# Causal attention and two gated products on one core: banks of the transposes and of the result, and the step at which the result is split

## The chip, the cores and the metric

The kernel runs on one core of a Trainium2 chip. The metric is the device time of one execution in microseconds (us): 584.55 us is the median of three runs before the change. TensorE (PE, with its weight loads as PEld), VectorE (DVE), ScalarE (ACT), GpSimd (POOL) and SyncE (SP, which issues the DMAs) each have a queue of their own and work through it in the order in which the program wrote it.

## The reference

Two batches, 12 heads, 448 tokens, head dimension 64; all in float32.

```python
scores = scale * (q @ k.T)                    # per head, causal mask
attn   = exp(scores - max) / (sum + 1e-9)
x      = concat_heads(attn @ v)               # 896 x 768
h = x @ w_in;  g = h * cos(h);  y = g @ w_out           # 768 -> 2048 -> 768
c = (y @ w_a) * (y @ w_b);      out = c @ w_out2        # 768 -> 1536 -> 768
```

## The kernel before

**Products.** Each large product is computed from activations and weights that are split into a high and a low part (`x_hi`, `x_lo` and so on), three matmuls for a term. They fill the time from about 90 us to the end.

**Attention.** The twelve units of work are pairs of heads, numbered 0 to 11 here (six pairs in each batch). A pair is done in four banks of scores (`BANKS`): the first holds tiles 6 and 0 (448 and 64 columns), the second tiles 4 and 2 (320 and 192), the third tile 5 (384), the fourth tiles 3 and 1 (256 and 128). One bank is one step of a loop that is written out by hand: `CYCLE` names each function with the step, counted from the pair's own, at which it is issued, and within a step the functions are issued in the order of the list. No scheduler moves anything after that.

For pair n, with its first step at 4n, the functions are:

- `scores` (L339, TensorE): matmuls of two banks, two steps ahead. Tile 6 (448 columns, first bank) comes first and tile 4 (320 columns, second bank) next.
- `row_max` (L362, VectorE): reads a bank of scores, adds the mask, writes the scores into one of two buffers `p` (`N_P = 2`, L298) and takes the row maximum. It frees the bank. Behind each stands a short read of the accumulator (`mn`).
- `exps` (L383, ScalarE): exponentials in `p`, with row sums. `recip` (L390, L391, VectorE): reciprocals of the sums. `scale_p` (L398, GpSimd): multiplies the rows.
- `transposes(n, odd)` (L412, TensorE): seven transposes of 128x128 into two banks, four in the first and three in the second; the even group at step 4n+5, the odd one at 4n+7.
- `keep(n, odd)` (L423 ScalarE, L425 VectorE): copies both banks into `pp`, one bank on each of the two engines.
- `values(n)` (L439, TensorE) at step 4n+10: the product with `v` into the bank `xa`.
- `x_hi(n)` (L449, ScalarE) and `x_lo(n)` (L454, VectorE): split `xa` into its high and its low part; `x_lo` is the last to read the bank.

The weights of the first product are prepared at fixed steps between these (L100, L105, L111, L118 and, on GpSimd, L129 and L138).

The eight banks of the accumulation memory are shared out by `BUFS`: four for scores (`s`), two for transposes (`t`), two for the result (`x`). The products later take all eight in turn, in the order of the tags.

Of the kernel before, what the change touches and what calls it, by code (L numbers as in the profile page):

```python
# [26 lines left out]
def tile_causal_attention_cos_gate_bilinear(  # L27
# [35 lines left out]
    def act_tiles(pool, tag, kind, b, n):  # L63
        return [
            tuple(pool.tile([P, S], F32R, tag=f"{tag}{b}_{t}{part}", name=f"{kind}{b}_{t}{part}") for part in ("hi", "lo"))
            for t in range(n)
        ]
# [89 lines left out]
    x = [act_tiles(xy, "xy", "x", b, NPAIR) for b in range(B)]  # L157

    psum = ctx.enter_context(tc.tile_pool(name="psum", bufs=1, space=PSUM))
    BUFS = {"s": 4, "t": 2, "x": 2}  # L160
    cycle = itertools.cycle([tag for tag, n in BUFS.items() for _ in range(n)])

    def bank(tag, name):
        return psum.tile([P, 512], F32, tag=tag, name=name, bufs=BUFS[tag])

# [113 lines left out]
    with ExitStack() as actx:  # L279
# [183 lines left out]
        def at(fn, i):  # L463
# [15 lines left out]
            (values, 10),  # L479
            (transposes, 5, 0),  # L480
            (transposes, 7, 1),
            (x_hi, 12),
            (x_lo, 13),
            (load_qk, -10),
            (load_v, -2),
        ]
# [131 lines left out]
```

## Time and profile before

| | |
|---|---|
| Runs | 584.55 us median of 3 (584.34 to 584.56) |
| Profiled execution | 584.54 us, of which the span of the trace is 582.7 |
| TensorE busy | 573.5 us, 98% of the span |
| VectorE, ScalarE, GpSimd busy | 360.7, 267.0, 221.4 us |
| TensorE clock granted | full in every slice |

Times of rows count from the start of the span. A busy time says that instructions were in flight on an engine; matmuls are pipelined, and where one waits while another is still in flight the row stays busy. "[0.66 <-POOL p L398]" behind a row says that the engine stood idle for 0.66 us before it, until the named instruction let it go on.

### The profile page before, as it was taken

What the parts mean: (1) busy time and instruction counts of PE and PEld (TensorE: products, weight loads), DVE (VectorE), ACT (ScalarE), POOL (GpSimd) and SP (SyncE); (2) the same over time, 40 slices, a digit from 0 to 9 for tenths busy, and PEclk for the clock granted to TensorE, in tenths of its full rate; (3) what the DMA queues carried; (4) which work ended last, traced back from release to release, by engine and by line L of the source; (5) the groups of instructions that cost most, each with busy time, mean ns of one, the idle gap of its engine ahead of it and who ended that gap; (6) DMA issues with size and microseconds to landing.
All of it is one profiled execution on the core that took longest, in us unless ns stands there. A gap on an engine that the chain in (4) does not pass through costs nothing.

```text
span 582.7 us, 8735 instructions
## 1 busy us (share of the span) xinstructions
PE 573.5 (98%) x3310; PEld 513.1 (88%) x3310; DVE 360.7 (62%) x599; ACT 267.0 (46%) x531; POOL 221.4 (38%) x200
## 2 busy tenths in 40 slices
PE   8899999999999999999999999999999999999997
PEld 6566688999999999999999999999999999999996
DVE  4888765777777774654465666666666666655400
ACT  5797847777777733232223433333333333222100
POOL 4756662666666652232132222222222222322200
PEclk9999999999999999999999999999999999999999
DMA  8671511233333334423242333333333333444000
GB/s 312 263 220 58 183 44 67 87 117 114 114 103 99 100 109 137 144 91 109 91 162 102 117 109 109 108 109 108 110 108 110 109 109 109 139 141 139 33 33 32
DMA packets 15450, 67.80 MB, mean 116 GB/s; under 512 B 1712, under 2 KB 3376, under 8 KB 15408
## 3 DMA queue, kind: packets, MB, share of 16 engines
q1 hardware_dynamic: 15408, 67.25, 34.4%
q8 instruction: 26, 0.43, 0.3%
q14 instruction: 16, 0.13, 0.1%
HBM read 64.49 MB, written 2.75 MB: 115 GB/s over the span
## 4 chain that ended last, share of the span: by engine, by line
PE 94%; DVE 2%; ACT 2%; POOL 1%; issue 1%; DVEq 0%; POOLq 0%
PE h L175 20%; PE y L175 20%; PE o L175 15%; PE a L175 15%; PE b L175 15%; PE xa L439 3%; PE pt L412 3%; PE s L339 2%; ACT p L383 2%; DVE p L362 1%; PE warm L459 1%; POOL p L398 1%; DVE pp L425 0%; POOL w_lo L138 0%; DVE w_raw L118 0%
## 5 line engine op out<-in xcount | busy, mean ns | idle before, releaser
L138 POOL TENSOR_TENSOR w_lo<-w_raw,w_hi 128x768 fp32r<-128x768 f32 (+1 forms) x70 | 128.9, 1841 | 264.8 <-ACT w_hi L131 194.1
L111 DVE SCALAR_TENSOR_TENSOR w_raw<-w_raw 128x768 int32<-128x768 int32 (+1 forms) x70 | 124.1, 1772 | 63.2 <-ACT w_raw L100 62.3
L131 ACT ACTIVATE w_hi<-w_raw 128x768 fp32r<-128x768 f32 (+1 forms) x67 | 59.9, 895 | 163.2 <-DVE w_raw L118 100.0
L118 DVE SCALAR_TENSOR_TENSOR w_raw<-w_raw 128x768 int32<-128x768 int32 (+1 forms) x70 | 65.9, 941 | 0.4
L100 ACT ACTIVATE w_raw<-w_raw 128x768 f32<-128x768 f32 (+1 forms) x70 | 61.4, 877 | 0.0
L398 POOL TENSOR_SCALAR p<-p,sums 128x448 f32<-128x448 f32 (+6 forms) x84 | 42.5, 527 | 27.3 <-DVE sums L391 16.9
L383 ACT ACTIVATE p<-p,mn 128x448 f32<-128x448 f32 (+6 forms) x84 | 41.8, 499 | 15.7 <-DVE mn L362 15.7
L105 DVE TENSOR_SCALAR w_raw<-w_raw 128x768 int32<-128x768 int32 (+1 forms) x70 | 42.7, 610 | 0.0
L362 DVE CUSTOM_DVE_ANT_0 p<-s,mask 128x448 f32<-128x448 f32 (+6 forms) x84 | 31.9, 416 | 13.1 <-PE pt L412 8.0
L215 DVE SCALAR_TENSOR_TENSOR r<-k,h 128x448 f32<-128x448 int32 x32 | 19.7, 617 | 26.0 <-ACT k L214 25.6
L568 DVE COPY o<-o 128x448 f32<-128x448 f32 x12 | 7.5, 625 | 35.3 <-PE o L175 35.3
L339 PE MATMUL s<-qk_raw 64*64 64x64 f32 (+6 forms) x336 | 28.5, 410 | 0.3 <-DVE mn L362 0.2
L412 PE MATMUL pt<-ident,p 128*128 128x128 f32 x168 | 23.7, 279 | 3.9 <-POOL p L398 2.2
L214 ACT ACTIVATE k<-h 128x448 int32<-128x448 f32 x32 | 17.3, 539 | 18.5 <-PE h L175 17.7
L339 PEld LDWEIGHTS s<-qk_raw 64*64 64x64 f32 x336 | 15.7, 139 | 11.3 <-issue 4.4
L412 PEld LDWEIGHTS pt<-ident,p 128*128 128x128 f32 x168 | 18.1, 140 | 7.5 <-POOL p L398 3.1
L560 DVE TENSOR_TENSOR c<-a,bs 128x448 f32<-128x448 f32 x24 | 15.0, 625 | 15.4 <-PE a L175 15.4
L439 PE MATMUL xa<-pp,v 128*64 128x64 f32 (+3 forms) x336 | 23.8, 293 | 0.0
L439 PEld LDWEIGHTS xa<-pp,v 128*64 128x64 f32 x336 | 16.1, 137 | 8.7 <-issue 6.8
L231 DVE SCALAR_TENSOR_TENSOR r<-r,h 128x448 f32<-128x448 f32 x32 | 19.5, 610 | 1.5 <-ACT r L226 1.5
L221 ACT ACTIVATE r<-r 128x448 f32<-128x448 f32 x32 | 18.3, 571 | 0.0
L226 ACT ACTIVATE r<-r 128x448 f32<-128x448 f32 x32 | 18.2, 569 | 0.0
(377 smaller groups left out, 1564.6 us busy)
## 6 DMA issues: line engine op xcount, KB each, us to landing
w_raw<-in_w_in SPq DMA_DIRECT2D x16, 768.0 KB, 4.3
w_raw<-in_w_out SPq DMA_DIRECT2D x12, 768.0 KB, 4.3
w_raw<-in_w_b SPq DMA_DIRECT2D x12, 768.0 KB, 4.2
w_raw<-in_w_a SPq DMA_DIRECT2D x12, 768.0 KB, 4.3
w_raw<-in_w_o SPq DMA_DIRECT2D x12, 768.0 KB, 4.3
v<-in_v SPq DMA_DIRECT2D x12, 448.0 KB, 5.4
qk_raw<-in_qk SPq DMA_DIRECT2D x11, 448.0 KB, 5.7
w_raw<-in_w_out SPq DMA_DIRECT2D x6, 512.0 KB, 3.8
```

Source lines behind the costliest of these rows:

```text
L100: nc.scalar.activation(high, high, ACTF.Copy, scale=2.0**-112)
L105: nc.vector.tensor_single_scalar(low, low, 29, op=ALU.logical_shift_right)
L111: nc.vector.scalar_tensor_tensor(out=low, in0=high, scalar=3, in1=low, op0=ALU.logical_shift_left, op1=ALU.bitwise_or)
L118: nc.vector.scalar_tensor_tensor(out=low, in0=high, scalar=SIGN, in1=low, op0=ALU.bitwise_and, op1=ALU.bitwise_or)
L131: nc.scalar.activation(pair[0][:, :n], src, ACTF.Copy)
L138: engine.tensor_tensor(out=lo[:, :n], in0=f32(raw.pop(i)[:, :, 0]), in1=f32(hi)[:, :n], op=ALU.subtract)
L175: nc.tensor.matmul(ps, w[:, c * P : (c + 1) * P], acts[t + c][part], start=t == 0 and i == 0, stop=t + k == n and i == len(terms) - 1,)
L339: nc.tensor.matmul(T["s", i + c][q, o : o + WIDTH[j]], t[h, Q_COL[j] : Q_COL[j] + D], t[h, FIRST[j] : FIRST[j] + WIDTH[j]], start=True, st ...
L383: nc.scalar.activation(t, t, ACTF.Exp, bias=T["mn", n][:, c], scale=-1.0, accum_out=row_sum(n, j))
L398: nc.gpsimd.tensor_scalar(out=t, in0=t, scalar1=row_sum(n, j), scalar2=1.0, op0=ALU.mult, op1=ALU.mult)
L412: nc.tensor.transpose(dst, p_bufs[n % N_P][:, o : o + P], ident)
L439: nc.tensor.matmul(ps[e * D : (e + 1) * D, o * D : w * D], t[:, k, e], p[:, :, :, q].rearrange("p s l q -> p (s l) q") if k < 3 else p[:, ...
```

## The change

One bank moves from the result to the transposes, and both halves of the split are issued one step sooner.

```diff
-    BUFS = {"s": 4, "t": 2, "x": 2}
+    BUFS = {"s": 4, "t": 3, "x": 1}
...
             (transposes, 5, 0),
             (transposes, 7, 1),
-            (x_hi, 12),
-            (x_lo, 13),
+            (x_hi, 11),
+            (x_lo, 12),
```

VectorE, around the row maxima of pair 5 (`p1_116`, scores `s_501` and the next bank) before the change; `pt_550` is the second bank of pair 3's odd transposes, `x0_2lo` the low part of pair 2's result:

```order
L391 RECIPROCAL sums_498<-sums_498 128x3
L425 COPY pp_512<-pt_550 128x3x128
L362 ISA p1_116,mn_554<-s_501,mask_101 128x320
L362 ISA mn_554 128x1
L362 ISA p1_116,mn_554<-s_501,mask_101 128x192
L362 ISA mn_554 128x1
L454 TENSOR_TENSOR x0_2lo_76<-xa_516,x0_2hi_75 128x448
L362 ISA p1_116,mn_554<-s_558,mask_101 128x384
```

The same place on VectorE after the change:

```order
L391 RECIPROCAL sums_498<-sums_498 128x3
L425 COPY pp_512<-pt_550 128x3x128
L454 TENSOR_TENSOR x0_2lo_76<-xa_516,x0_2hi_75 128x448
L362 ISA p1_116,mn_555<-s_501,mask_101 128x320
L362 ISA mn_555 128x1
L362 ISA p1_116,mn_555<-s_501,mask_101 128x192
L362 ISA mn_555 128x1
L362 ISA p1_116,mn_555<-s_559,mask_101 128x384
```

The low part has moved from behind the row maxima of 320 and 192 columns to a place ahead of them, right behind the copy of the transposes. The same holds for every pair that has row maxima there.

ScalarE at the same pair before the change (`pt_545` is the first bank of pair 3's odd transposes):

```order
L383 ACTIVATE p0_115,sums_498<-p0_115,mn_462 128x128
L423 ACTIVATE pp_512<-pt_545 128x4x128
L383 ACTIVATE p1_116,sums_555<-p1_116,mn_554 128x448
L383 ACTIVATE p1_116,sums_555<-p1_116,mn_554 128x64
L449 ACTIVATE x0_2hi_75<-xa_516 128x448
L383 ACTIVATE p1_116,sums_555<-p1_116,mn_554 128x320
```

And after it:

```order
L383 ACTIVATE p0_115,sums_498<-p0_115,mn_463 128x128
L449 ACTIVATE x0_2hi_75<-xa_516 128x448
L423 ACTIVATE pp_512<-pt_545 128x4x128
L383 ACTIVATE p1_116,sums_556<-p1_116,mn_555 128x448
L383 ACTIVATE p1_116,sums_556<-p1_116,mn_555 128x64
L383 ACTIVATE p1_116,sums_556<-p1_116,mn_555 128x320
```

The high part now stands ahead of the copy of the odd transposes and of two exponentials.

TensorE's queue holds the same instructions in the same order; what an instruction waits for has changed. Pair 2's even transposes before the change (`Activation_49`, `DVE_49`, `Pool_49` and `PE_49` are the counters of ScalarE, VectorE, GpSimd and TensorE):

```order
L412 MATMUL pt_488<-ident_66,p1_116 128x2x64 [waits Activation_49,Pool_49]
L412 MATMUL pt_488<-ident_66,p1_116 128x2x64
L412 MATMUL pt_488<-ident_66,p1_116 128x128
L412 MATMUL pt_488<-ident_66,p1_116 128x2x64
L412 MATMUL pt_493<-ident_66,p1_116 128x128 [waits DVE_49,PE_49]
```

And after it:

```order
L412 MATMUL pt_489<-ident_66,p1_116 128x2x64 [waits Pool_49]
L412 MATMUL pt_489<-ident_66,p1_116 128x2x64
L412 MATMUL pt_489<-ident_66,p1_116 128x128
L412 MATMUL pt_489<-ident_66,p1_116 128x2x64
L412 MATMUL pt_494<-ident_66,p1_116 128x128 [waits Activation_49]
```

The first transpose no longer waits for a copy, only for the scaled rows; the fifth waits for ScalarE's copy instead of VectorE's.

## Rows read from the trace of the kernel before

**Rows 1.** Busy time by stretches: stretch, its length, busy time (instructions) of PE first

```profile
30.00:40.00 10.00, 10.00 (x124) 7.03 (x124) 8.57 (x38) 9.18 (x33) 6.34 (x14) 1.00 0.77 252
...
90.00:580.00 490.00, 488.63 (x2417) 452.53 (x2413) 295.65 (x338) 203.51 (x323) 168.89 (x99) 1.00 0.32 105
```

**Rows 2.** Waits of PE: for whom, us in total, times, longest

```profile
PE pt L412 <- POOL p L398: 2.2, 3, 0.9
PE pt L412 <- ACT pp L423: 1.0, 2, 0.5
...
PE pt L412 <- DVE pp L425: 0.6, 2, 0.4
```

**Rows 3.** Timeline of PE, from pair 3's odd transposes to pair 4's

```profile
33.97 0.98 PE L412 MATMUL pt<-ident,p 128*128 128x128 f32 x7
...
36.66 1.23 PE L339 MATMUL s<-qk_raw 64*64 64x448 f32 x16
...
37.82 1.98 PE L439 MATMUL xa<-pp,v 128*64 128x384 f32 x28
...
39.73 0.98 PE L412 MATMUL pt<-ident,p 128*128 128x128 f32 x7
```

**Rows 4.** Score matmuls (L339) in flight, PE first; pairs 4, 6 and 11

```profile
25.20:25.28 0.08, 0.00 (x1) 0.01 (x1) 1.00 1.83 768
25.20:25.30 0.10, 0.02 (x4) 0.03 (x4) 1.00 1.46 614
...
36.68:36.80 0.12, 0.12 (x2) 0.12 (x4) 1.00 0.38 149
36.80:36.82 0.02, 0.02 (x4) 0.02 (x4) 1.00 0.88 358
...
68.12:68.23 0.11, 0.11 (x2) 0.11 (x4) 1.00 0.00 0
68.23:68.25 0.02, 0.02 (x4) 0.02 (x4) 1.00 0.00 0
```

**Rows 5.** Timeline of DVE in the same turn

```profile
35.10 0.22 DVE L362 CUSTOM_DVE_ANT_0 p<-s,mask 128x64 f32<-128x64 f32 x1 [1.09 <-PE pt L412]
...
35.54 0.53 DVE L425 COPY pp<-pt 128x384 f32<-128x384 f32 x1
...
35.98 0.48 DVE L362 CUSTOM_DVE_ANT_0 p<-s,mask 128x320 f32<-128x320 f32 x1
...
36.67 0.08 DVE L362 DVE_READ_ACCUMULATOR2_ANT mn<- 128x1 f32 x1
36.70 0.62 DVE L454 TENSOR_TENSOR x_2lo<-xa,x_2hi 128x448 fp32r<-128x448 f32 x1
...
37.24 0.55 DVE L362 CUSTOM_DVE_ANT_0 p<-s,mask 128x384 f32<-128x384 f32 x1
```

**Rows 6.** Timeline of DVE ahead of pair 11's scores

```profile
68.10 0.08 DVE L362 DVE_READ_ACCUMULATOR2_ANT mn<- 128x1 f32 x1
```

**Rows 7.** Timeline at pair 9's scores: DVE and PEld

```profile
55.90 0.08 DVE L362 DVE_READ_ACCUMULATOR2_ANT mn<- 128x1 f32 x1
...
56.03 0.73 PEld L339 LDWEIGHTS s<-qk_raw 64*64 64x64 f32 x12 [0.82 <-DVE mn L362]
```

**Rows 8.** Timeline of ACT in the same turn as rows 3

```profile
34.66 0.60 ACT L423 ACTIVATE pp<-pt 128x512 f32<-128x512 f32 x1 [0.39 <-PE pt L412]
...
36.14 0.53 ACT L449 ACTIVATE x_2hi<-xa 128x448 fp32r<-128x448 f32 x1
...
36.56 0.55 ACT L383 ACTIVATE p<-p,mn 128x320 f32<-128x320 f32 x1
```

**Rows 9.** Timeline of PE: a wait for a copy

```profile
48.09 0.95 PE L412 MATMUL pt<-ident,p 128*128 128x128 f32 x7 [0.51 <-ACT pp L423]
```

**Rows 10.** Timeline of POOL and PE in pair 9's turn

```profile
55.38 0.90 POOL L129 TENSOR_SCALAR w_hi<-w_raw 128x768 fp32r<-128x768 f32 x1 [2.57 <-DVE w_raw L118]
...
59.65 0.98 PE L412 MATMUL pt<-ident,p 128*128 128x128 f32 x7 [0.62 <-POOL p L398]
```

## The prediction

> **What bounds the kernel now.** I read the busy time by stretches first. From 90 us to the end the matrix products keep TensorE busy for 488.63 of 490 us, and the attention's middle, 30 to 40 us, reads 10.00 of 10 [rows 1]. The change touches the attention alone (its first 90 us) and the rotation of the banks, so what it is worth must be read there. Next I read the waits of TensorE: before transposes 2.2 us on GpSimd, 1.0 on ScalarE and 0.6 on VectorE, the last two on the copies that free a transpose bank (L423, L425) [rows 2]. That is all that the profile itself calls a wait for a bank: 1.6 us.
>
> A full row need not be an engine that never waits, so the third view is the timeline of one pair. Transposes of one pair and the next start at 33.97 and 39.73: 5.76 us a pair [rows 3]. Inside it the score matmuls of pair 6 start at 36.66. They go to two banks, and tile 4 (320 columns, the second bank) runs beside tile 6 (448, the first) in the other quarter of the array. Compare how late tile 4 starts [rows 4]. In pair 4 all four matmuls of tiles 6 and 4 begin between 25.28 and 25.30. In pair 6 only tile 6's two run up to 36.80, and tile 4's two begin between 36.80 and 36.82, 0.14 us after tile 6's. Pair 11 does the same: two until 68.23, four after. The cause is on VectorE: tile 4's bank is free when the row maxima of 320 and 192 columns of the pair before have been read, whose last instruction ends at 36.67 + 0.08 = 36.75, and at 68.10 + 0.08 = 68.18 in pair 11 [rows 5, 6]. Each time tile 4 starts 0.05 to 0.07 us later. In pair 9 the wait is long enough to be shown: VectorE ends at 55.98, the weight load starts at 56.03 with 0.82 us idle before it "<-DVE mn" [rows 7]. Behind tile 4 the rest follows without a gap: in pair 6 the values start 37.82 - 36.81 = 1.01 us after it [rows 3, 4]. So VectorE, not TensorE, sets the pace, though TensorE's row is full.
>
> The whole ring can be followed: the odd transposes end; VectorE may now overwrite the score rows that they read (two buffers, L298) and starts the 64-column row maximum at 35.10, 1.09 us idle, "<-PE pt"; reciprocals; copy of the odd transposes at 35.54; the two row maxima from 35.98, done at 36.75 [rows 5]; then tile 4, the values at 37.82 and the next odd transposes at 39.73 [rows 3]. Whatever is put between the copy and the row maximum lengthens every turn.
>
> **The change part by part.**
>
> *The split's second half (x_lo, L454) one step sooner.* The order of VectorE shows it directly behind that copy and ahead of the two row maxima that tile 4 waits for; before, it stood behind them. Its slot on VectorE is measured: it starts at 36.70 and the next instruction at 37.24, 0.54 us (its own duration is 0.62, its tail overlaps) [rows 5]. Lower bound 0, were there slack between the row maximum and tile 4; the rows leave none in pairs 6, 9 and 11. Upper bound 0.62, its full duration. I take 0.54. What it brings back: VectorE's place behind the row maxima is free, so the 384-column maximum starts as before after the transposes; but the exponentials of 320 and 192 columns come 0.54 later on ScalarE, and the reciprocal behind the 384 waits for them. That later delay falls into VectorE's idle 1.09 us before the next 64-column maximum [rows 5], which has moved by the same 0.54, so it costs nothing more.
>
> How many pairs pay: x_lo of pair n stands ahead of the row maxima of pair n+3, which free the bank for the scores of pair n+4. That makes pairs 4 to 11, eight. Pair 4 had no delay of tile 4 [rows 4], so I count it at zero. Pairs 5 to 11 are seven: 7 x 0.54 = 3.8 us. Two of them are paced by more than the ring. In pair 9's turn VectorE also prepares a weight, GpSimd waits 2.57 us for that and TensorE 0.62 us for GpSimd [rows 10]. There x_lo now also stands ahead of that weight instruction (L118), so GpSimd's chain moves by the same 0.54, and I count the pair in full.
>
> *The split's first half (x_hi, L449) one step sooner.* ScalarE now does it before the copy of the odd transposes. That copy waited 0.39 us for TensorE (34.66), and x_hi's slot is 36.56 - 36.14 = 0.42 us [rows 8], so it fits into the idle time to within 0.03. Its input, the values, ends before those transposes begin, since TensorE does them in that order. x_lo finds it done. Cost: 0 taken; if that idle time were gone, 0.42 a pair.
>
> *Three banks for the transposes.* The first four transposes of a group now find a free bank; from the fifth on they wait for one copy. The waits it can shorten are the 1.6 us [rows 2]. The one at 48.09 is 0.51 us, for ScalarE's copy [rows 9], and no single one is longer [rows 2]. They lie where the other engines set the pace: behind them tile 4 waits for VectorE's row maxima anyway, so earlier transposes only lengthen that wait. I take 0, bounds 0 and -1.6.
>
> *One bank for the result.* The values of pair n must wait until x_lo of pair n-1 has read the bank. x_lo is now ahead of the row maxima, tile 4 waits for those, and the values stand behind tile 4 on TensorE: no wait of its own, 0. Had x_lo stayed, it ended at 36.70 + 0.62 = 37.32, still ahead of 37.82 [rows 3, 5].
>
> *The products.* Eight banks are used in turn before and after, and each comes round after eight products. With 1.4 us idle in 490 [rows 1] there is nothing to gain or to absorb: 0, so that what the attention loses reaches the end.
>
> Sum against the profiled execution (584.54 us, its span 582.7 and 1.84 around it; the median of the runs is 584.55): 584.54 + 3.8 = 588.3 us.
>
> **The rivals.**
>
> *Hidden in VectorE's idle time.* VectorE idles 1.09 us a pair [rows 5], twice x_lo's slot, so the move could cost nothing: 584.5. Against it: that idle time lies ahead of the 64-column maximum, before the copy, and x_lo is behind the copy, where VectorE runs on without a gap up to 36.75. It decides only if tile 4 has over 0.54 us to spare, as perhaps in pair 4.
>
> *Faster: the transposes' banks were the bound.* If the waits for copies vanish and x_lo is hidden too: 584.54 - 1.6 = 582.9. For it speaks that these waits stand in the trace [rows 2, 9]; against it that in the steady pairs the transposes wait for nothing. It decides from the point where tile 4's wait after such a stall is shorter than the stall; in pair 9 that wait was 0.82 us [rows 7], more than any of them. The Trainium skill (Perfetto Trace Analysis, Optimization Strategy) says that the same gap repeating on the engine that should be saturated can mean too few PSUM buffers. By that rule the third bank helps, with the 582.9 of this rival; the trace does show a repeating gap, but its releaser is the row maximum, whose four banks stay as they are.
>
> *Fewer pairs pay.* If the two turns with weight work (pairs 8 and 9) swallow the slot, 5 x 0.54 = 2.7, 587.2; less one bank wait of 0.51, 586.7.
>
> *More.* If ScalarE's 0.39 us are not there when x_hi needs them, up to 0.42 more a pair: 588.3 + 7 x 0.42 = 591.2. With x_lo at its full 0.62 in all eight pairs: 584.54 + 5.0 = 589.5.
>
> **How the numbers follow.** Forecast 0.72 (its own range 587.5 to 589.5); fewer pairs 0.10; ScalarE late 0.05; hidden 0.08; faster 0.05. The predicted time is 588.3. A range of 586.7 to 589.5 holds the first two, 0.82. Runs of this kernel can tell about 0.2% (1.2 us) from no change: slower 0.72 + 0.10 + 0.05 = 0.87, same 0.08, faster 0.05.
>
> **What the changed profile would show.** Right: about 6.30 us from one pair's odd transposes to the next's; x_lo between the copy and the 320-column maximum; the 320 matmuls some 0.7 us after the 448, now long enough to appear as TensorE idle "<-DVE mn"; ScalarE waiting before the 320-column exponential; the products start some 3.8 us later and last as long. Wrong: 5.76 us a pair with x_lo in its new place (tile 4 had slack), transposes waiting for ScalarE in every pair (x_hi too dear), values waiting for VectorE (the single bank), or a product stage of another length.

## The result and the profile after

The changed kernel takes 587.79 us (median of 4 runs, 587.37 to 588.39), against 584.55; the ratio is 1.0061 with a 95% interval of 1.0049 to 1.0073. It is slower by 0.6%.

The timeline of TensorE in the changed kernel, from pair 3's odd transposes to pair 4's, answers to [rows 3]:

```profile
34.05 0.98 PE L412 MATMUL pt<-ident,p 128*128 128x128 f32 x7
...
36.69 1.81 PE L339 MATMUL s<-qk_raw 64*64 64x448 f32 x16
38.43 1.98 PE L439 MATMUL xa<-pp,v 128*64 128x384 f32 x28
40.34 0.33 PE L412 MATMUL pt<-ident,p 128*128 128x128 f32 x1
```

A pair takes 40.34 - 34.05 = 6.29 us instead of 5.76. All of it lies in the score matmuls, whose row grew from 1.23 to 1.81 us with the same 16 instructions (the even transposes ahead of them took 0.05 us less). The row still reads as busy. The view of the score matmuls in flight (as [rows 4]: stretch, its length, busy time and instructions of PE, then of PEld) shows what is in it:

```profile
36.68:37.40 0.72, 0.71 (x4) 0.20 (x4) 1.00 0.79 182
37.40:37.44 0.04, 0.04 (x4) 0.02 (x2) 1.00 0.22 90
```

Tile 6's matmuls stand alone for 0.72 us, four of them, with no weight load after the first ones. The timeline of the weight loads names what the next one, tile 4's, waited for:

```profile
37.42 0.73 PEld L339 LDWEIGHTS s<-qk_raw 64*64 64x64 f32 x12 [0.53 <-DVE mn L362]
```

Before, tile 4 joined 0.14 us after tile 6. The timeline of VectorE in this turn, as [rows 5], has the cause:

```profile
35.18 0.22 DVE L362 CUSTOM_DVE_ANT_0 p<-s,mask 128x64 f32<-128x64 f32 x1 [1.16 <-PE pt L412]
...
35.62 0.53 DVE L425 COPY pp<-pt 128x384 f32<-128x384 f32 x1
36.07 0.61 DVE L454 TENSOR_TENSOR x_2lo<-xa,x_2hi 128x448 fp32r<-128x448 f32 x1
36.60 0.48 DVE L362 CUSTOM_DVE_ANT_0 p<-s,mask 128x320 f32<-128x320 f32 x1
...
37.28 0.08 DVE L362 DVE_READ_ACCUMULATOR2_ANT mn<- 128x1 f32 x1
```

From the release by the transposes to the end of the second row maximum it was 36.75 - 35.10 = 1.65 us, and is 37.36 - 35.18 = 2.18: the 0.53 us (36.60 - 36.07) of x_lo's slot. VectorE's idle time ahead of the 64-column maximum is as long as before, 1.16 against 1.09.

On ScalarE x_hi went where the idle time was, and the exponential behind the delayed row maximum now waits:

```profile
34.20 0.52 ACT L449 ACTIVATE x_2hi<-xa 128x448 fp32r<-128x448 f32 x1
34.74 0.60 ACT L423 ACTIVATE pp<-pt 128x512 f32<-128x512 f32 x1
...
37.12 0.56 ACT L383 ACTIVATE p<-p,mn 128x320 f32<-128x320 f32 x1 [0.80 <-DVE mn L362]
```

The waits of TensorE, as [rows 2], are fewer for copies, as the banks would suggest, and more for row maxima:

```profile
PE pt L412 <- POOL p L398: 2.2, 3, 0.9
PE s L339 <- DVE mn L362: 1.7, 2, 1.0
...
PE pt L412 <- DVE pp L425: 0.3, 1, 0.3
```

The third transpose bank did take away waits for copies, 1.6 us down to 0.3, and the kernel became slower all the same. Last, the chain of work that ended last, behind the attention, in the changed kernel (start, length, what):

```profile
93.66 109.02 PE h L175 x537
202.68 116.74 PE y L175 x576
```

Before, the same pieces took 109.03 and 116.74 us. The products are untouched and only start later.

### The profile page after: what moved, and what is told of

Read it like the earlier page. It is cut to its first block, busy times and chain, and to the rows that moved or that the text cites. A ratio compares the mean times of both kernels' runs of the same rounds, so it can differ in the third digit from the quotient of the medians.

```text
span 586.2 us, 8726 instructions
## 1 busy us (share of the span) xinstructions
PE 576.7 (98%) x3310; PEld 512.8 (87%) x3310; DVE 361.0 (62%) x599; ACT 268.3 (46%) x531; POOL 221.2 (38%) x200
## 4 chain that ended last, share of the span: by engine, by line
PE 94%; DVE 3%; ACT 1%; POOL 1%; issue 1%; DVEq 0%; POOLq 0%
PE h L175 20%; PE y L175 20%; PE o L175 15%; PE a L175 15%; PE b L175 15%; PE xa L439 3%; PE s L339 3%; PE pt L412 3%; ACT p L383 1%; DVE p L362 1%; PE warm L459 1%; DVE pp L425 0%; POOL p L398 0%; POOL w_lo L138 0%; DVE w_raw L118 0%
## 5 line engine op out<-in xcount | busy, mean ns | idle before, releaser
L111 DVE SCALAR_TENSOR_TENSOR w_raw<-w_raw 128x768 int32<-128x768 int32 (+1 forms) x70 | 124.0, 1772 | 63.2 <-ACT w_raw L100 62.4
L105 DVE TENSOR_SCALAR w_raw<-w_raw 128x768 int32<-128x768 int32 (+1 forms) x70 | 42.7, 609 | 0.0
L339 PE MATMUL s<-qk_raw 64*64 64x320 f32 (+6 forms) x336 | 31.3, 396 | 1.7 <-DVE mn L362 1.7
L339 PEld LDWEIGHTS s<-qk_raw 64*64 64x64 f32 x336 | 15.2, 134 | 15.3 <-DVE mn L362 7.3
```

Of the source, the lines that this page charges most:

```text
L105: nc.vector.tensor_single_scalar(low, low, 29, op=ALU.logical_shift_right)
L111: nc.vector.scalar_tensor_tensor(out=low, in0=high, scalar=3, in1=low, op0=ALU.logical_shift_left, op1=ALU.bitwise_or)
L339: nc.tensor.matmul(T["s", i + c][q, o : o + WIDTH[j]], t[h, Q_COL[j] : Q_COL[j] + D], t[h, FIRST[j] : FIRST[j] + WIDTH[j]], start=True, st ...
```

## The experiments

Ratios are against the kernel before, run beside them on the same chip (584.1 to 584.2 us there). x_hi and x_lo are the first and second half of the split.

**One part at a time.** Banks alone:

```diff
-    BUFS = {"s": 4, "t": 2, "x": 2}
+    BUFS = {"s": 4, "t": 3, "x": 1}
```

> The banks of the change (three for transposes, one for the result), the split at its old steps. Theory, the second half of the split lengthens VectorE's ring and the banks cost nothing: 584.5 us, tile 4's score matmuls 0.14 us after tile 6's as before. Rival, the single result bank or the shared transpose banks cost the time: 587.8 us.

Measured: 584.10 us, ratio 0.9999 (0.9989 to 1.0008). The banks cost nothing, and the waits that they shorten are worth nothing. The trace shows where they went. The view of its waits lists none of the 1.6 us for copies any more, but the waits of score matmuls for row maxima grew; in the kernel before and in this one:

```profile
PE s L339 <- DVE mn L362: 0.2, 1, 0.2
PE s L339 <- DVE mn L362: 1.2, 2, 0.7
```

In a steady turn the even transposes end 0.05 us sooner, and the row of score matmuls is 0.05 us longer (1.23 before); tile 4 starts some 0.2 us after tile 6, not 0.14 as expected:

```profile
36.58 1.28 PE L339 MATMUL s<-qk_raw 64*64 64x448 f32 x16
```

Steps alone:

```diff
-            (x_hi, 12),
-            (x_lo, 13),
+            (x_hi, 11),
+            (x_lo, 12),
```

> The split one step sooner, the banks as before (two and two). Theory: 587.8 us, all of the change's loss, 6.29 us a pair. Rival, the banks cost the time: 584.5 us.

Measured: 588.44 us, 1.0074 (1.0059 to 1.0089); its odd transposes start at 33.56 and 39.85, 6.29 us apart. The steps carry the whole loss. Against the kernel before beside it that is 4.2 us, 1.0 more than the change lost. In the traces the seven turns are equally long (73.85 - 27.27 = 46.58 us from pair 2's odd transposes to pair 9's, 46.60 in the change); behind them 0.5 us more is lost (93.62 - 73.85 = 19.77 us to the products, against 93.66 - 74.36 = 19.30), where transposes wait 0.51 us for VectorE's copy. So with the split moved, the third bank gives about that much back.

Banks and x_hi, x_lo where it was:

```diff
             (x_hi, 11),
-            (x_lo, 12),
+            (x_lo, 13),
```

(shown against the changed kernel)

> The change with its second half (x_lo) back at the old step; x_hi sooner and the banks stay. Theory: 584.5 us, since ScalarE does x_hi in the 0.39 us in which it waited for transposes. Rival, ScalarE ahead of its copy costs something: 586 us or more, with transposes waiting for ScalarE.

Measured: 583.92 us, 0.9998 (0.9989 to 1.0007). x_hi costs nothing; moving the one line of x_lo is the loss.

**The same work twice, in both places.** Against the changed kernel, and, for the old place, the same edit against the kernel before:

```diff
-            nc.vector.tensor_tensor(out=lo, in0=T.pop(("xa", n))[:, :S], in1=f32(hi), op=ALU.subtract)
+            ps = T.pop(("xa", n))[:, :S]
+            for _ in range(2):
+                nc.vector.tensor_tensor(out=lo, in0=ps, in1=f32(hi), op=ALU.subtract)
```

> The change with x_lo issued twice in a row in its new place (the second writes the same values). Theory: one more slot of 0.54 us in each of seven turns, 587.8 + 3.8 = 591.6 us, 6.83 us a pair. Rival, the place costs once whatever stands in it, since VectorE idles 1.1 us a pair: 587.8 us.

Measured: 593.34 us, 1.0159 (1.0144 to 1.0174), 5.5 us above the change where 3.8 were expected. The timeline of VectorE shows why it is more (the inserted lines move the line numbers: x_lo is L456 here). The second row is the second x_lo by itself:

```profile
36.98 1.27 DVE L456 TENSOR_TENSOR x_2lo<-xa,x_2hi 128x448 fp32r<-128x448 f32 x2
37.63 0.62 DVE L456 TENSOR_TENSOR x_2lo<-xa,x_2hi 128x448 fp32r<-128x448 f32 x1
38.17 0.48 DVE L362 CUSTOM_DVE_ANT_0 p<-s,mask 128x320 f32<-128x320 f32 x1
```

And that of TensorE:

```profile
34.97 0.98 PE L412 MATMUL pt<-ident,p 128*128 128x128 f32 x7
...
37.61 0.97 PE L339 MATMUL s<-qk_raw 64*64 64x448 f32 x4
38.99 1.08 PE L339 MATMUL s<-qk_raw 64*64 64x320 f32 x12 [0.42 <-DVE mn L362]
...
41.92 0.33 PE L412 MATMUL pt<-ident,p 128*128 128x128 f32 x1
```

Two in a row take 38.17 - 36.98 = 1.19 us, so a second x_lo adds 0.66 and not 0.54; a pair takes 6.95 us. Six of the seven turns grew by 0.63 to 0.66 us, pair 9's by 0.30 (8.49 against 8.19): 4.2 us in all, from 78.84 - 28.02 = 50.82 against 46.60. Pair 4, which had time to spare for one slot, pays 0.4 for the second (its tile 4 starts at 25.1, with tile 6 from 24.66 on). The other 0.8 lies behind the last turn (98.93 - 78.84 = 20.09 us to the products, against 19.30), where transposes wait 0.65 us for VectorE's copy. In this place work costs its full slot in all turns but pair 9's. The wait is at last long enough to be shown on TensorE's row: tile 6's matmuls are in flight for 0.97 us, and tile 4 starts 1.38 us after them.

> The kernel before with x_lo issued twice in a row in its old place, behind the row maxima. Theory: VectorE's idle 1.09 us ahead of the 64-column row maximum takes the slot: 584.5 us, that idle time about 0.55 us. Rival, any work added to VectorE lengthens the pair: 588.3 us.

Measured: 585.88 us, 1.0030 (1.0019 to 1.0041), between the two. In the steady turns the theory holds: VectorE's idle time ahead of the 64-column maximum fell to 0.43 us and paid for the whole slot; the odd transposes start at 27.44 and 33.20, 5.76 us apart as before. (The row names GpSimd, but the maximum starts 1.13 us after those transposes, as it did before: 34.33 - 33.20 and 35.10 - 33.97.)

```profile
34.33 0.22 DVE L362 CUSTOM_DVE_ANT_0 p<-s,mask 128x64 f32<-128x64 f32 x1 [0.43 <-POOL p L398]
...
36.08 1.29 DVE L456 TENSOR_TENSOR x_2lo<-xa,x_2hi 128x448 fp32r<-128x448 f32 x2
```

The time went where a weight is prepared in the same turn. At 47.50 the 64-column maximum followed the 448-column one with no idle time at all, behind 0.76 and 0.96 us of weight work (L105, L111). There is nothing there to pay from: the odd transposes before and after it start at 44.78 and 52.37, 7.59 us apart, against 51.98 - 45.49 = 6.49 in the kernel before: the slot, and 0.39 us that x_lo waited for x_hi ahead of it (at 42.19). Another 0.9 us went behind the last turn (91.29 - 71.37 = 19.92 us to the products, against 90.21 - 71.16 = 19.05), where a weight is prepared too and transposes wait 0.66 us for ScalarE's copy; pair 9's turn was 0.2 us shorter.

**Into the idle time itself.** Against the changed kernel, x_lo between the two row maxima of the first bank:

```diff
             for j in BANKS[b]:
 
+                if b == 0 and j == 0:
+                    x_lo(n - 3)
```

(with a test in `x_lo` that leaves the later call without work)

> The change with x_lo issued still sooner, between the row maxima of 448 and 64 columns, where VectorE waits for the odd transposes. Theory: its input ends at about 34.7 in pair 5's turn, its slot at 35.25, against 35.10 at which the transposes let VectorE go on: 0 to 0.2 us a pair, 584.5 to 586 us. Rival, sooner is dearer wherever it stands: 587.8 us.

Measured: 586.69 us, 1.0041 (1.0026 to 1.0056); above the range, and below the rival. VectorE in a steady turn and in pair 8's:

```profile
34.87 0.63 DVE L458 TENSOR_TENSOR x_2lo<-xa,x_2hi 128x448 fp32r<-128x448 f32 x1 [0.73 <-ACT x_2hi L451]
35.42 0.21 DVE L364 CUSTOM_DVE_ANT_0 p<-s,mask 128x64 f32<-128x64 f32 x1
...
48.56 0.62 DVE L458 TENSOR_TENSOR x_4lo<-xa,x_4hi 128x448 fp32r<-128x448 f32 x1 [0.73 <-ACT x_4hi L451]
```

In the steady turn most of x_lo is hidden: the odd transposes start at 34.18 and 40.03, 5.85 us apart. In pair 8's turn, where VectorE had no idle time, it first waits 0.73 us for x_hi and then takes its slot: 53.72 - 46.20 = 7.52 us, against 6.49 before. So the slot was cheap where there was idle time, and the wait for its input, which my expectation had only for the steady turn, made it dear elsewhere.

**Opening the ring.** Against the changed kernel:

```diff
-        N_P = 2
+        N_P = 3
```

> The change with three score-row buffers instead of two, so that the 64-column row maximum needn't wait for the odd transposes just issued. Theory: the ring is open, VectorE runs ahead, and the slot of x_lo costs nothing: 583.6 us (584.5 less 7 x 0.13 that tile 4 waited before), tile 4 within 0.02 us of tile 6. Rival, the slot costs whatever closes the ring: 587.8 us.

Measured: 584.46 us, 1.0002 (0.9993 to 1.0012): the loss is gone, but not the 0.9 us beyond it. The 64-column maximum no longer waits. The turn now begins at the copy of the transposes:

```profile
34.99 0.56 DVE L425 COPY pp<-pt 128x384 f32<-128x384 f32 x1 [0.38 <-PE pt L412]
35.46 0.61 DVE L454 TENSOR_TENSOR x_2lo<-xa,x_2hi 128x448 fp32r<-128x448 f32 x1
```

The ring had a second closing, the copy itself, which my expectation forgot; x_lo still stood behind it. So the kernel before got the same third buffer:

> The kernel before with three score-row buffers. With three buffers in the change VectorE's turn still began at the copy of the odd transposes, and x_lo behind it kept tile 4 waiting 0.21 us. Here x_lo stands behind the row maxima, so the turn is 0.54 us shorter. Theory: tile 4 within 0.02 us of tile 6, some 5.63 us a pair, 0.13 less than before in seven pairs: 583.3 us. Rival, TensorE's own pace is 5.76 us a pair: 584.2 us.

Measured: 582.86 us, 0.9979 (0.9970 to 0.9988). The odd transposes start at 33.20 and 38.77, 5.57 us apart, and tile 4 starts with tile 6 (four in flight by 35.87, where the row starts at 35.84). Better than expected by 0.4 us: TensorE's own pace is 5.57 us, not 5.63, so the kernel before lost about 0.18 us a pair to the same row maxima (three pairs: 45.49 - 28.21 = 17.28 us against 44.35 - 27.62 = 16.73).

**Shortening the ring.** The banks of the change, the split at its old steps, and the copies of the odd transposes behind the row maxima:

```diff
-            (keep, 8, 1),
+            (keep, 9, 1),
```

> The change's banks, the split at its old steps, and the copies of the odd transposes one step later, behind the row maxima of 320 and 192 columns. Theory: VectorE's ring is 0.44 us shorter than before, tile 4 no longer waits, 583.6 us (7 x 0.13 less than before). Rivals: TensorE sets the pace anyway, 584.5 us; or ScalarE's copy, now behind two exponentials, keeps the fifth transpose waiting, 586 us or more.

Measured: 586.41 us, 1.0039 (1.0024 to 1.0054): the second rival. Tile 4 starts with tile 6, but the fifth transpose waits for ScalarE's copy:

```profile
37.02 0.55 PE L412 MATMUL pt<-ident,p 128*128 128x128 f32 x3 [0.43 <-ACT pp L423]
```

So only VectorE's copy was moved:

```diff
-            (keep, 8, 1),
+            (keep, 8, 1, True),
+            (keep, 9, 1, False),
...
+                if only not in (None, bool(on_act)):
+                    continue
```

> The change's banks, the split at its old steps, and only VectorE's copy of the odd transposes one step later, behind the row maxima of 320 and 192 columns; ScalarE's copy stays where it was, ahead of the exponentials. Theory: VectorE's turn is 0.44 us shorter than before and the fifth transpose no longer waits for ScalarE, as it did when both copies moved: tile 4 within 0.02 us of tile 6, 5.63 us a pair, 583.3 us. Rival, TensorE's own pace is 5.76 us a pair, or the copy is missed by the transposes: 584.2 us or more.

Measured: 582.72 us, 0.9974 (0.9964 to 0.9985), with two buffers of score rows. TensorE's timeline:

```profile
33.38 0.98 PE L412 MATMUL pt<-ident,p 128*128 128x128 f32 x7
...
36.02 1.09 PE L339 MATMUL s<-qk_raw 64*64 64x448 f32 x16
37.04 1.98 PE L441 MATMUL xa<-pp,v 128*64 128x384 f32 x28
38.95 0.98 PE L412 MATMUL pt<-ident,p 128*128 128x128 f32 x7
```

The score matmuls take 1.09 us (1.23 before, 1.81 with the change) and a pair 5.57.

The same with the old banks (`{"s": 4, "t": 2, "x": 2}`):

> VectorE's copy of the odd transposes later, with two banks each for transposes and result as before the change. Theory: the fifth even transpose now waits for that copy, which ends at 36.16 where the fifth would start at 35.6, so about 0.55 us in each of eight pairs: 587 us; the third transpose bank is what makes the later copy possible. Rival, the bank count does not matter here either: 582.7 us.

Measured: 589.44 us, 1.0083 (1.0069 to 1.0097). The timeline of TensorE has the wait at the size expected, and the view of its waits (total, times, longest) ten of them:

```profile
37.81 0.52 PE L412 MATMUL pt<-ident,p 128*128 128x128 f32 x3 [0.55 <-DVE pp L427]
...
PE pt L412 <- DVE pp L427: 7.1, 10, 1.8
```

The median lies 2.4 us above the 587 expected, and the runs differ by TensorE's granted clock. In two of the six, the traced one among them, its mean is 1.000, and they take 587.6 us; in the other four it is 0.994 to 0.997, lower than in any other run here (0.998 and more), and they take 589.2 to 590.06. Where the clock fell in those four, and why, no trace shows. By the two runs at 1.000 the third bank is worth 587.6 - 582.72 = 4.9 us here; the median's 6.7 us holds the lower clock as well. Alone the bank gives nothing, but it lets the copy be late.

Both remedies together:

> VectorE's copy of the odd transposes later, the change's banks, and three score-row buffers as well. Theory: each of the two alone brought the steady pairs to TensorE's own pace (5.57 us), so together they gain there nothing; only the two turns with weight work (pairs 8 and 9) can be shorter: 582.2 to 582.8 us. Rival, the gains add: 581.4 us.

Measured: 582.12 us, 0.9966 (0.9953 to 0.9979), just under the range, by 0.1 us. It is the fastest of all, 1.9 us below the kernel before and 5.7 below the change. In the traces only pair 9's turn got shorter by it, from 58.38 - 51.18 = 7.20 to 57.11 - 50.75 = 6.36 us; pair 8's stayed (6.66 and 6.67).

## Why the prediction was right

**The time.** 588.3 was predicted, 587.79 measured, inside the range. The loss of the medians is 3.2 us where 3.8 were forecast. In the two traces the products start 93.66 - 90.21 = 3.45 us later, although the changed execution had its first scores sooner: its first row maximum starts at 5.99 and not at 6.45. From there on the loss is 3.9 us. The seven turns that were counted hold 3.65 of it: from pair 2's odd transposes to pair 9's it is 71.16 - 28.21 = 42.95 us before and 74.36 - 27.76 = 46.60 after. The other 0.25 lies behind the last turn, where the weight loads of pair 11's even transposes wait:

```profile
83.47 0.31 PEld L412 LDWEIGHTS pt<-ident,p 128*128 128x128 f32 x3 [0.24 <-DVE pp L425]
```

The sum did not have that, so that 3.9 and 3.8 agree so closely is in part luck. Whether the sooner start also makes the medians' loss smaller was not shown: each kernel has one trace.

**The ring.** That VectorE and not TensorE paced the pairs, although TensorE read 10.00 of 10 us, was right. The experiments show it both ways: x_lo once more in that place lengthens six of the seven turns by what it takes on VectorE, and a shorter VectorE turn (later copy) or one that starts sooner (third buffer, x_lo at the old step) makes the pairs faster than before.

**The size per turn.** 0.54 us taken from the slot, 0.53 measured in a steady pair (6.29 - 5.76). Pair 4 was rightly counted at nothing: its scores lie between the odd transposes of pairs 1 and 2, and these start 28.21 - 21.64 = 6.57 us apart before and 27.76 - 21.20 = 6.56 after.

**The turns with weight work.** Pairs 8 and 9 were counted in full, and they paid: from the odd transposes of pair 5 to those of pair 7 it is 59.65 - 45.49 = 14.16 us before and 61.78 - 46.63 = 15.15 after, 0.5 us for each.

**x_hi, the banks, the products.** Each was taken at zero, and the runs with the banks alone and with x_hi alone agree, as do the lengths of the products. The faster rival's waits were real and did vanish, 1.6 to 0.3 us, without any gain; with the banks alone tile 4 waited longer by what the transposes had gained, as the prediction said. Of the rule on repeating gaps (the Trainium skill, Perfetto Trace Analysis, Optimization Strategy) the trace shows a limit: tile 4's wait repeated in every steady pair, without a gap in TensorE's row, but it was let go by a row maximum, and more transpose banks did not touch it. Only after the order on VectorE had been changed did the third bank count for more than 0.5 us. That row maximum frees a bank of scores, and a fifth bank for scores (in place of the second for the result) was not tried, so for those banks the rule stays open.

**What was off.** The prediction called 1.6 us all that the profile calls a wait for a bank; the view has one wait more, 0.2 us of score matmuls for a row maximum (shown above with the banks alone), which is a wait for a bank of scores. The expectations of the third buffer and the later copy took tile 4's 0.13 us as all that the ring cost before; the faster versions show 0.18 a pair. And the prediction said in passing that the wait would be long enough to appear as TensorE's idle time. Of the seven turns only pair 9's shows it (0.99 us, at 58.19; the other of the two in the view is at 18.27, ahead of them). In the rest tile 4 starts 0.63 to 0.73 us after tile 6, whose own matmuls are in flight for 0.97.

## What to carry to other kernels

Follow one turn of the loop from a release on one engine to the next release on it, and ask of every moved instruction whether it now stands inside that ring; idle time of its engine helps only if it lies behind the new place. A full TensorE row is no proof that TensorE paces a stage: compare how late the second group of matmuls starts in a turn that waits and one that doesn't. A spare bank or buffer is worth what the order of the instructions lets it be: the third transpose bank gave nothing alone, and 4.9 us under a copy that was moved behind the critical row maxima.

## What the runs showed that was not expected

The same instruction twice in a row on VectorE took 1.19 us: the second started 37.63 - 36.98 = 0.65 us after the first, while the next instruction of another kind started 0.54 us after the second. Both write the same tile; whether that is the reason was not tested. And a wait of tile 4 leaves no gap in TensorE's busy row until it starts 0.97 us after tile 6, since tile 6's own matmuls are in flight meanwhile: of the twelve waits of score matmuls for row maxima that the weight loads show in the changed kernel (7.3 us in all), the matmul row shows two.

```profile
PEld s L339 <- DVE mn L362: 7.3, 12, 1.8
```

The start differs by up to 0.9 us between the traces, though no edit moves an instruction ahead of it: VectorE's first row maximum, which waits for the first scores, started at 6.45 us before, 5.99 with the change, 5.83 with both remedies and 5.55 with the steps alone. What moves it stays open.

```profile
5.99 0.63 DVE L362 CUSTOM_DVE_ANT_0 p<-s,mask 128x448 f32<-128x448 f32 x1 [4.59 <-PE s L339]
```

So where two traces are compared to 0.1 us here, it is from a point behind that start.
